# Even units regrouped in a fused attention loop: scores, one dV quarter, gradient products, then o and dQ; q transposes for dK in halves

## The chip, the cores and the metric

The kernel runs on one core of a Trainium2 chip. The metric is device time in microseconds (us): 1098.23 us, the median of three runs of the kernel before (1097.64 to 1101.65).

## The reference, cut to what matters

The reference returns the output of two attention blocks side by side and the gradients of all inputs for a given `grad_out`. Block A is linear attention. Block B, whose work fills the loop that is changed, is softmax attention with 16 query heads of width 28 that share one key and one value head, over 2048 tokens:

```python
q = (x @ wq).reshape(B, S, H, Dh)     # transposed to heads first
k = x @ wk
v = x @ wv
scores = jnp.einsum("bhqd,bkd->bhqk", q, k) * (Dh ** -0.5)
p = _softmax(scores, axis=-1)
o = jnp.einsum("bhqk,bkd->bhqd", p, v)
...                                    # o @ wo, and the vjp of all of it for grad_out
```

So the loop needs, for each pair of heads and each stretch of queries, the exponentiated scores, o, the product of the gradient of o with v, the gradient of the scores (dS), and from these dQ, dK and dV.

## The kernel before

A first stage of about 205 us does block A and the projections of block B. The loop in the middle does the attention of block B, and a last stage of about 40 us does the remaining weight and input gradients.

**Tiling of the loop.** A *block* b (64 of them) is a pair of heads with 256 queries; eight blocks share one query chunk `qc`. A *unit* u (512 of them, `NU`) is an eighth of a block: two tiles of 128 keys (t2 = 0, 1), both heads (h = 0, 1). The loop runs over u and is written under `tc.manual_schedule()`, so every engine and every queue runs its instructions in the order in which the loop writes them. A unit works on several stages at once, on older and older data:

- `rows_SD` (lines 683 to 705): score products S of unit u into two of three banks `SB`, and products D of the gradient with v for unit w = u - 16 into the two banks `DB`. Each has four matmuls of 32 rows. They lie on different rows of the TensorE array: 32 rows each for S of h = 0 and 1 and for D of h = 0 and 1.
- ScalarE: `eT` = exp(S) for h = 0 (line 939), the copy `cp` of D for h = 1 (line 953), exp(S) for h = 1 (line 985), in this order.
- VectorE: `dsT` = D * eT for h = 0 (line 951), and the 32x32 transpose `dsx` of the dsT of unit u - 18 (line 1023). GpSimd: dsT = cp * eT for h = 1 (line 954).
- The SyncE queue (SP): in every odd unit one DMA transpose of two units of `eT` into `eN` (line 988), 16 blocks of 128x128. The ring `ETs` holds 20 units, `ENs` 24.
- TensorE, at the end of a unit: in odd units `dk_m` (dK, 32 matmuls on 32x32 tiles, with `dsx` and `qX`), in even units `o_dq` (o of units u - 2, u - 1 and dQ of units u - 20, u - 19, 16 matmuls) and after it `dv_mm` (dV). `dv_mm` (line 894) does a quarter of a block's dV, eight matmuls that read `eN` of the whole block. For block b the quarters 0 and 1 come in unit 8b + 20, quarter 2 in 8b + 22, quarter 3 in 8b + 24, and none in 8b + 26.
- Every eight units there are a few more: `onat_T`, `o_norm`, `row_D`, `don_T`, `don_copy`, and a slice of the output projection (`out_proj`), which borrow the third SB bank (`spare`).

**q for dK.** For each query chunk from 1 to 7, `qc_copy` (line 842, GpSimd) spreads a group of q rows into the one buffer `qst` in two copies, and `qc_T` (line 847, SP queue) transposes it into `qX`, 8 blocks of 128x128. This happens four times per 64 units, for u mod 64 in 30 to 58: the copies are written in units 30 and 31, 38 and 39, 46 and 47, 54 and 55, and `qc_T` at the end of units 31, 39, 47 and 55, behind that unit's `eN` transpose. Since `qst` is one buffer, the copies of units 38, 46 and 54 wait until the DMA of the `qc_T` before has landed.

**The first twenty units.** `do_proj` and `do_copy` do the first ten row tiles of the gradient projection in units 1, 3, ..., 19. Units below 16 use a DB bank, 17 and 19 the bank `dk_acc`, which dV and dK use from unit 20 on.

Of the kernel before, what the change touches and what calls it, by code (L numbers as in the profile page):

```python
# [17 lines left out]
P = 128  # L18
# [7 lines left out]
def kernel(  # L26
# [21 lines left out]
    nc = tc.nc  # L48
# [31 lines left out]
    def mm(out_ap, lhsT, rhs, start=True, stop=True):  # L80
        nc.tensor.matmul(out_ap, lhsT=lhsT, rhs=rhs, start=start, stop=stop, tile_position=(0, 0))  # L81
# [565 lines left out]
    NB = 64  # L647
# [3 lines left out]
    with ExitStack() as cs_:  # L651
# [10 lines left out]
        DB = [psA.tile([P, 512], F32, name="agen") for i in range(2)]  # L662
        oq, dk_acc = (psA.tile([P, 512], F32, name="agen") for _ in range(2))

        dsT, dsx, qX, don, doT, rl, prod = ({} for _ in range(7))
# [3 lines left out]
        def eT(u):  # L669
            return ETs[u // 4 % 5][:, u % 4, :, :]  # L670

        def eN(b, c):
            return ENs[(2 * b + c // 2) % 6][:, 16 * (c % 2):16 * (c % 2) + 16, :]

        def mmt(out, lhsT, rhs, pos, start, stop):
            nc.tensor.matmul(out, lhsT=lhsT, rhs=rhs, start=start, stop=stop, tile_position=pos,  # L676
                             skip_group_check=True)

        def blk(b):
            qc, pair = divmod(b, 8)  # L680
            return qc, pair, pair // 2, pair % 2

        def rows_SD(u, sp, dp):
            b, tp = divmod(u, 8)
            w = u - 16
            qc, pair, g, hp = blk(b)
            todo = [(0, 0), (0, 1), (1, 0), (1, 1)] * 2
            if sp is not None and dp is not None and u % 2 == 0:
                todo = [(0, 0), (0, 1), (1, 0)] * 2 + [(1, 1)] * 2
            seen = {}  # L690
            for d in todo:
                if (dp if d[0] else sp) is None:
                    continue
                k, h = d
                t2 = seen.get(d, 0)
                seen[d] = 1
                t = 2 * tp + t2
                tc_ = slice(t * P, (t + 1) * P)
                oc = slice(t2 * 256, (t2 + 1) * 256)
                r = 64 * (1 - hp if k else hp) + 32 * h  # L700
                if k:
                    mmt(dp[h][:, oc], vT_rep[r:r + 32, tc_], doT[w // 8][r:r + 32, :], (r, 0), True, True)
                else:
                    mmt(sp[h][:, oc], kT_rep[r:r + 32, tc_], qT_B[g][r:r + 32, qc * 256:(qc + 1) * 256],
                        (r, 0), True, True)
# [3 lines left out]
        qst = pp_.tile([P, 8, 4, 32], BF16, name="qst", bufs=1)[:, :, :, :]  # L709
# [85 lines left out]
        def due(u, lag):  # L795
            b, r = divmod(u - lag, 8)
            return b if r == 0 and 0 <= b < NB else None
# [46 lines left out]
            eng.tensor_copy(out=st.rearrange("p (b s) a j -> p b s a j", s=2)[:, :, s, :, :],  # L844
                            in_=src.unsqueeze(2).to_broadcast([P, 4, 4, 32]))

        def qc_T(st, qc, g):
            nc.sync.dma_start_transpose(qX[qc].rearrange("p b s c -> p (b s) c")[:, :, g * P:(g + 1) * P],
                                        st.rearrange("p n a j -> p (n a j)"))

        KH = 256
        kv_acc = [dk_acc]
# [1 line left out]
        def dk_quad(a, x):  # L854
            return 32 * ((a + 2 * x) % 4)

        def dk_m(b, m):
            qc, pair, g, hp = blk(b)
            h, B, s = m // 8, (m // 2) % 4, m % 2
            for x in range(2):  # L860
                for a in range(4):
                    rhs = dsx[b][32 * a:32 * a + 32, 4 * x:4 * x + 4, h, :, :].rearrange(
                        "p u t (b i s) -> p u t b i s", b=4, s=2)[:, :, :, B, :, s]
                    k = dk_quad(a, x)
                    mmt(kv_acc[x][k:k + 32, 0:KH],
                        qX[qc][32 * a:32 * a + 32, B, s, pair * 64 + 32 * h:pair * 64 + 32 * h + 32],
                        rhs, (32 * a, k), False, b == NB - 1 and m == 15)
# [19 lines left out]
        def o_dq(vs, ys):  # L887
            for v, y in zip(vs, ys):
                todo = [f(i) for f, i in ((o_mm, v), (dq_mm, y)) if 0 <= i < NU]
                for _ in range(2):  # L890
                    for g_ in todo:
                        next(g_)

        def dv_mm(b, h, qb):
            for x in range(2):
                for c in range(4):
                    rhs = eN(b, c).rearrange("p (u h t q) k -> p u h t q k", u=2, h=2, t=2)[:, x, h, :, qb, :]
                    mmt(kv_acc[x][32 * c:32 * c + 32, KH:512], don[b][:, qb, h, :], rhs, (0, 32 * c),
                        b == 0 and h + qb == 0, b == NB - 1 and h + qb == 2)

        def do_proj(i, c0, c1, ps):
            for c in range(4):
                mm(ps[:, 0:c1 - c0], gbT[:, i, c, :], woTp[:, c, c0:c1], start=(c == 0), stop=(c == 3))
# [1 line left out]
        def do_copy(i, c0, c1, ps):  # L905
            nc.vector.tensor_copy(out=do_nat[:, i, c0:c1], in_=ps[:, 0:c1 - c0])

        do_slots = {2 * i + 1: (i, 0, 512) for i in range(10)}
        do_slots.update({37 + 8 * (n // 2) + 2 * (n % 2): (10 + n // 4, n % 4 * P, n % 4 * P + P) for n in range(24)})
        with tc.manual_schedule():  # L910
            nc.sync.dma_start(wo, wo_d[:, 0:D].rearrange("(g p) c -> p g c", p=P))
            qX[0] = pqa_.tile([P, 4, 2, 512], BF16, name="qX")
            for g in range(4):
                st = pd_.tile([P, 2, 512], BF16, name="dsT").rearrange("p a (n j) -> p a n j", j=32).rearrange(
                    "p a (n b) j -> p (a n) b j", b=4)
                qc_copy(nc.gpsimd, st, 0, g, 0)
                qc_copy(nc.vector, st, 0, g, 1)
                qc_T(st, 0, g)
            for u in range(NU + 28):
                w = u - 16  # L920
                hasS = u < NU
                hasD = 0 <= w < NU
                sp = [SB[(2 * u + h) % 3] for h in range(2)] if hasS else None
                dp = DB if hasD else None
                spare = SB[(2 * u + 2) % 3] if hasS else DB[u // 4 % 2] if u > 530 else SB[2]
                rows_SD(u, sp, dp)
                if (b := due(u, 10)) is not None:
                    onat_T(b, spare)
                if (b := due(u, 14)) is not None:
# [2 lines left out]
                    out_proj(*op, spare)  # L932
                dpj = do_slots.pop(u, None)
                if dpj is not None:
                    dps_ = DB[u // 2 % 2] if u < 16 else dk_acc if u < 20 else spare
                    do_proj(*dpj, dps_)

                if hasS:
# [16 lines left out]
                gq, iq = divmod(u % 64 - 30, 8)  # L955
                qq = u // 64 + 1
# [11 lines left out]
                if (b := due(u, 27)) is not None:  # L968
                    qc, pair, g, hp = blk(b)
# [14 lines left out]
                if hasS:  # L984
                    nc.scalar.activation(out=eT(u)[:, 1, :], in_=sp[1][:, :], func=ACT.Exp, scale=scale)  # L985
                    if u % 2:
                        k = u % 4 - 1
                        nc.sync.dma_start_transpose(ENs[u // 4 % 6][:, 8 * k:8 * k + 16, :],
                                                    ETs[u // 4 % 5][:, k:k + 2, :, :].rearrange("p a b c -> p (a b c)"))
                    if 0 <= gq < 4 and iq == 1 and u < 448:  # L990
                        qc_T(qst, qq, gq)

                if u % 2:
                    b, i = divmod(u - 27, 8)
                    if 0 <= b < NB:
                        for m in range(2 * i, 2 * i + 4):
                            dk_m(b, m)
                else:
                    o_dq((u - 2, u - 1), (u - 20, u - 19))
                    b, n = divmod(u - 20, 8)  # L1000
                    for k in {0: (0, 1), 2: (2,), 4: (3,)}.get(n, ()) if 0 <= b < NB else ():
                        dv_mm(b, k // 2, k % 2)
                y = u - 18

                if 512 <= u < 528 and u % 2 == 0:
# [13 lines left out]
                if 0 <= y < NU:  # L1019
                    b, tp = divmod(y, 8)  # L1020
# [19 lines left out]
        for c in range(4):  # L1040
            for x in range(2):
                k = dk_quad(c, x)
# [100 lines left out]
```

## Time and profile before

| | |
|---|---|
| median of three runs | 1098.23 us |
| the profiled execution | 1102.18 us |
| its span, first to last instruction | 1100.4 us |
| mean granted TensorE clock | 0.973 |
| TensorE matmul busy | 1011.5 us (92%) |
| VectorE busy | 902.7 us (82%) |
| ScalarE busy | 879.3 us (80%) |
| GpSimd busy | 799.4 us (73%) |
| DMA packets of the SP and ACT transposes and copies (queue q1) | 684488, 179.99 MB |

The profiled execution took 3.95 us more than the median, and 1.8 us of it lie outside its span. The busy shares are averages over three stages; in the loop ScalarE and VectorE are above 90%. A matmul's end is modelled, so a busy TensorE is not one at its peak. The SP queue has no busy row on the page: its instructions only issue DMAs, and their durations stand in the timeline of that queue.

### The profile page before, as it was taken

To read this page: it belongs to the slowest core of one execution; us is meant where nothing else is said; L and a number is where in the kernel's file an instruction comes from. 1 tells how busy PE (TensorE), PEld (TensorE's weight loads), DVE (VectorE), ACT (ScalarE), POOL (GpSimd) and SP (SyncE) were. 2 spreads that over 40 slices of the span, in tenths; PEclk is the share of its full clock that TensorE was granted. 3 is DMA by queue.
4 is the path that set the end of the run, shared out by engine and by line. 5 is a ranking of instruction groups with operands and counts; after the bars stand their busy time and mean duration, and the time that the engine had idled before them with its cause. 6 is when DMAs were issued, how large, how long until landed. Compare 5 with 4: busy or idle time off the path is not lost.

```text
span 1100.4 us, 49383 instructions
## 1 busy us (share of the span) xinstructions
PE 1011.5 (92%) x20717; PEld 555.8 (51%) x20717; DVE 902.7 (82%) x1794; ACT 879.3 (80%) x1745; POOL 799.4 (73%) x1044
## 2 busy tenths in 40 slices
PE   9999999989999889989988998999899989999898
PEld 5655554444555545545554554455455544555444
DVE  7895503578999989989998998899899978999942
ACT  6553223799999989989998998899989978999532
POOL 8501451368888888878888888888898878888851
PEclk9999999999999999989999899899999989999999
DMA  9879998499999999999999999999999999999993
GB/s 259 151 146 189 204 213 165 91 173 177 181 179 175 180 185 179 175 182 187 171 181 182 182 186 178 175 186 184 175 178 189 172 185 184 185 169 178 225 169 91
DMA packets 693193, 195.77 MB, mean 178 GB/s; under 512 B 674505, under 2 KB 690785, under 8 KB 692969
## 3 DMA queue, kind: packets, MB, share of 16 engines
q1 hardware_dynamic: 684488, 179.99, 105.2%
q0 software_dynamic: 4544, 9.46, 3.4%
q10 hardware_dynamic: 3936, 3.16, 0.9%
q8 instruction: 162, 2.65, 0.9%
q14 instruction: 63, 0.51, 0.1%
HBM read 12.60 MB, written 10.84 MB: 21 GB/s over the span
## 4 chain that ended last, share of the span: by engine, by line
PE 35%; ACT 19%; issue 16%; DVE 16%; POOL 10%; SPq 2%; DMA 1%; DVEq 0%; ACTq 0%; POOLq 0%
PE agen L81 12%; ACT cp L953 10%; PE agen L676 8%; POOL dsT L954 8%; ACT eT L985 7%; PE aacc L676 6%; PE aacc L81 6%; DVE dsx L1023 5%; DVE dsT L951 4%; DVE oTs L967 2%; DVE oTs L812 1%; ACT eT L939 1%; PE aacc L833 1%; DVE rl L811 1%; SPq L1014 1%
## 5 line engine op out<-in xcount | busy, mean ns | idle before, releaser
L954 POOL TENSOR_TENSOR dsT<-cp,eT 128x512 bf16<-128x512 bf16 x512 | 587.7, 1157 | 79.2 <-ACT cp L953 72.4
L1023 DVE STREAM_TRANSPOSE dsx<-dsT 128x512 f32<-128x512 f32 x512 | 358.3, 700 | 24.4 <-POOL dsT L954 22.2
L676 PEld LDWEIGHTS <-R 32*128 32x128 bf16 (+1 forms) x8192 | 233.7, 94 | 285.6 <-issue 255.5
L951 DVE TENSOR_TENSOR dsT<-agen,eT 128x512 bf16<-128x512 f32 x512 | 342.4, 669 | 26.6 <-PE agen L676 20.8
L939 ACT ACTIVATE eT<-aacc 128x512 bf16<-128x512 f32 x512 | 311.5, 608 | 43.0 <-PE agen L676 30.9
L953 ACT ACTIVATE cp<-agen 128x512 bf16<-128x512 f32 x512 | 312.3, 610 | 23.0 <-PE agen L676 12.7
L985 ACT ACTIVATE eT<-aacc 128x512 bf16<-128x512 f32 x512 | 318.2, 621 | 0.0
L676 PE MATMUL aacc<-R,R 32*128 32x256 bf16 x2048 | 255.6, 280 | 32.6 <-DVE oTs L812 26.5
L676 PE MATMUL agen<-doT,R 32*128 32x256 bf16 x2048 | 272.1, 275 | 12.7 <-DVE dsT L951 2.8
L676 PE MATMUL agen<-dsT,R 128*32 128x256 bf16 x2048 | 165.3, 283 | 7.9 <-POOL dsT L954 7.7
L676 PE MATMUL aacc<-dsx,qX 32*32 32x256 bf16 x4096 | 170.2, 279 | 0.1
L676 PE MATMUL agen<-dsx,qX 32*32 32x256 bf16 x4096 | 169.8, 279 | 0.0
L676 PE MATMUL agen<-eT,R 128*32 128x256 bf16 x2048 | 164.3, 282 | 0.1
L676 PEld LDWEIGHTS <-qX 32*32 32x32 bf16 x8192 | 93.9, 90 | 55.6 <-issue 51.8
L81 PEld LDWEIGHTS <-R 128*128 128x128 bf16 x781 | 60.7, 97 | 59.3 <-issue 24.3
L676 PE MATMUL agen<-eN,don 128*32 128x256 bf16 x1024 | 80.3, 287 | 0.0
L676 PE MATMUL aacc<-eN,don 128*32 128x256 bf16 x1024 | 80.2, 286 | 0.0
L844 POOL COPY qst<-R 128x512 bf16<-128x512 bf16 x56 | 34.2, 611 | 50.5 <-DMA qX<-qst 50.5
L676 PEld LDWEIGHTS <-don 128*32 128x32 bf16 x2048 | 64.6, 102 | 3.4
L81 PE MATMUL agen<-R,R 128*128 128x448 bf16 (+1 forms) x168 | 39.0, 359 | 0.7 <-ACT R L229 0.4
L816 POOL TENSOR_TENSOR prod<-R,oTs 128x128 f32<-128x128 bf16 x64 | 27.6, 431 | 9.3 <-DVE oTs L812 9.3
L586 DVE TENSOR_TENSOR osb<-R 32x512 bf16<-32x512 bf16 x4 | 1.7, 413 | 34.9 <-ACT R L583 34.9
(237 smaller groups left out, 1010.1 us busy)
## 6 DMA issues: line engine op xcount, KB each, us to landing
eN<-eT SPq DMA_TRANSPOSE x256
xa<-in_A_x_dram SPq DMA_DIRECT2D x8, 224.0 KB
ga<-in_grad_out_dram SPq DMA_DIRECT2D x4, 448.0 KB
out_dram<-osb ACTq DMA_DIRECT2D x16, 112.0 KB
xa<-in_grad_out_dram POOLq DMA_DIRECT2D x4, 448.0 KB, 10.1
out_dram<-wdq POOLq DMA_DIRECT2D x8, 224.0 KB, 5.4
eT<-in_grad_out_dram SPq DMA_DIRECT2D x4, 448.0 KB
eT<-in_B_x_dram SPq DMA_DIRECT2D x4, 448.0 KB
```

What stands on the lines that cost most here:

```text
L81: nc.tensor.matmul(out_ap, lhsT=lhsT, rhs=rhs, start=start, stop=stop, tile_position=(0, 0))
L676: nc.tensor.matmul(out, lhsT=lhsT, rhs=rhs, start=start, stop=stop, tile_position=pos, skip_group_check=True)
L811: nc.vector.reciprocal(out=r_[:], in_=onp[:, :, :, 0:1])
L816: nc.gpsimd.tensor_tensor(out=prod[b][:], in0=dnv, in1=os_, op=ALU.mult)
L844: eng.tensor_copy(out=st.rearrange("p (b s) a j -> p b s a j", s=2)[:, :, s, :, :], in_=src.unsqueeze(2).to_broadcast([P, 4, 4, 32]))
L939: nc.scalar.activation(out=eT(u)[:, 0, :], in_=sp[0][:, :], func=ACT.Exp, scale=scale)
L951: nc.vector.tensor_tensor(out=dst[:, 0, :], in0=dp[0][:, :], in1=ew[:, 0, :], op=ALU.mult)
L953: nc.scalar.activation(out=cp[:, :], in_=dp[1][:, :], func=ACT.Copy)
L954: nc.gpsimd.tensor_tensor(out=dst[:, 1, :], in0=cp[:, :], in1=ew[:, 1, :], op=ALU.mult)
L967: nc.vector.tensor_copy(out=oTs[0:64, :], in_=oq[0:64, 0:256])
L985: nc.scalar.activation(out=eT(u)[:, 1, :], in_=sp[1][:, :], func=ACT.Exp, scale=scale)
L1023: nc.vector.transpose(out=dsx[b][:, tp, :, :, :].rearrange("p h t c -> p (h t c)").bitcast(F32), in_=dsT[y][:, :, :].rearrange("p h c -> p ...
```

## The change

In even units in which both S and D exist (u = 16 to 510), `rows_SD` is called twice: first for S alone, in the order h = 0, 1, 0, 1, then one quarter of dV, then `rows_SD` for D alone, 0, 1, 0, 1. Before, these units had the order S0 S1 D0, S0 S1 D0, D1 D1, and dV came last. The quarters of block b now lie one each in units 8b + 18, 20, 22 and 24 (`dv_due`). Odd units stay S0 S1 D0 D1, twice.

`qc_T` takes a range of the eight blocks. It is called twice per group, with four blocks each, at the end of the even units that follow by one and by three: 32 and 34, 40 and 42, 48 and 50, 56 and 58 (mod 64). The copies stay where they are.

In the first units, `do_proj` moves to 1, 3, 5, 7, 9, 11, 13, 14, 15, 17, with `dk_acc` in 14 and 17, so that `dk_acc` is free when dV begins in unit 18.

```diff
-            if sp is not None and dp is not None and u % 2 == 0:
-                todo = [(0, 0), (0, 1), (1, 0)] * 2 + [(1, 1)] * 2
...
-        def qc_T(st, qc, g):
-            nc.sync.dma_start_transpose(qX[qc].rearrange("p b s c -> p (b s) c")[:, :, g * P:(g + 1) * P],
-                                        st.rearrange("p n a j -> p (n a j)"))
+        def qc_T(st, qc, g, n0=0, n1=8):
+            nc.sync.dma_start_transpose(qX[qc].rearrange("p b s c -> p (b s) c")[:, n0:n1, g * P:(g + 1) * P],
+                                        st[:, n0:n1, :, :].rearrange("p n a j -> p (n a j)"))
...
+        def dv_due(u):
+            b, n = divmod(u - 18, 8)
+            if 0 <= b < NB:
+                dv_mm(b, n // 4, n // 2 % 2)
...
-        do_slots = {2 * i + 1: (i, 0, 512) for i in range(10)}
+        do_slots = {u: (i, 0, 512) for i, u in enumerate((1, 3, 5, 7, 9, 11, 13, 14, 15, 17))}
...
-                rows_SD(u, sp, dp)
+                split = hasS and hasD and u % 2 == 0
+                if split:
+                    rows_SD(u, sp, None)
+                    dv_due(u)
+                    rows_SD(u, None, dp)
+                else:
+                    rows_SD(u, sp, dp)
...
-                    dps_ = DB[u // 2 % 2] if u < 16 else dk_acc if u < 20 else spare
+                    dps_ = dk_acc if u in (14, 17) else DB[u // 2 % 2] if u < 16 else spare
...
-                    if 0 <= gq < 4 and iq == 1 and u < 448:
-                        qc_T(qst, qq, gq)
+                    if 0 <= gq < 4 and iq in (2, 4) and u < 448:
+                        qc_T(qst, qq, gq, 2 * iq - 4, 2 * iq)
...
-                    b, n = divmod(u - 20, 8)
-                    for k in {0: (0, 1), 2: (2,), 4: (3,)}.get(n, ()) if 0 <= b < NB else ():
-                        dv_mm(b, k // 2, k % 2)
+                    if not split:
+                        dv_due(u)
```

## The prediction

> **What bounds the kernel now.** I read the page first. ScalarE and VectorE stand at 80% and 82% of the span, but the loop is only three quarters of it. The table by stretch gives the loop, here one stretch outside and one inside the units that prepare q for dK. Columns: length, then busy us of TensorE, weight loads, VectorE, ScalarE, GpSimd, the granted clock, DMA share, GB/s.
>
> ```profile
> 308.50:357.40 48.90, 45.00 (x1200) 26.16 (x1192) 47.58 (x96) 48.03 (x96) 42.10 (x51) 1.00 1.23 181
> 571.00:620.00 49.00, 43.31 (x1068) 23.08 (x1068) 43.05 (x83) 43.39 (x86) 40.18 (x49) 0.90 1.17 175
> ```
>
> In the first, ScalarE is busy for 48.03 of 48.90 us and eight units take 12.2 us. In the second, ten instructions of ScalarE fewer fit into the same time. From the starts of line 939, the stretches of eight units from u mod 64 = 40, 48 and 56 take 15.4, 13.1 and 13.8 us, all others 12.1 to 12.3: 5.7 us lost per 64 units, 40 us over seven chunks. What is waited for there is in the groups and the timeline:
>
> ```profile
> L844 POOL COPY qst<-R 128x512 bf16<-128x512 bf16 x56 | 34.2, 611 | 50.5 <-DMA qX<-qst 50.5
> ```
>
> ```profile
> 601.86 0.61 POOL L844 COPY qst<-R 128x512 bf16<-128x512 bf16 x1 [2.77 <-DMA qX<-qst]
> ...
> 603.62 0.71 DVE L1023 STREAM_TRANSPOSE dsx<-dsT 128x512 f32<-128x512 f32 x1 [1.23 <-POOL dsT L954]
> ...
> 605.99 0.60 ACT L939 ACTIVATE eT<-aacc 128x512 bf16<-128x512 f32 x1 [1.29 <-DVE dsx L1023]
> ```
>
> GpSimd waits for the landing of the transpose that read `qst` (21 times, 2.4 us on average), VectorE then for GpSimd, ScalarE for VectorE. Of the 50.5 us, 40 are lost. So why is that DMA late? The copies of units 30 and 31 end at 561.5 us, their transpose is issued at 570.1, with ScalarE in unit 38. The SP queue's own timeline says why:
>
> ```profile
> 574.62 9.63 SPq L988 DMA_TRANSPOSE eN<-eT  x3
> 584.35 1.26 SPq L848 DMA_TRANSPOSE qX<-qst  x1
> 585.71 11.54 SPq L988 DMA_TRANSPOSE eN<-eT  x4
> 597.34 1.50 SPq L848 DMA_TRANSPOSE qX<-qst  x1
> 598.95 11.22 SPq L988 DMA_TRANSPOSE eN<-eT  x4
> 610.26 2.05 SPq L848 DMA_TRANSPOSE qX<-qst  x1
> ```
>
> There is no gap. From unit 30 to 510 transposes fill 743.8 of 773.7 us, and most of the rest is the 0.1 us between two. Each `eN` transpose is issued 5 to 11 us, mostly 8, after its exp has ended. This **lag** neither grows nor vanishes. In stretches without `qX`, one `eN` transpose takes 3.02 us of the queue (12 of them in 36.2 us), the compute 3.05 us per two units: about even. A `qX` transpose adds 1.40 us (the stretch from unit 29 to 65 holds 18 and four, 59.96 us). So the queue needs 32 x 3.02 + 4 x 1.40 = 102.2 us per 64 units, with the few transposes of line 976 about 103; the compute alone needs 97.6; the loop takes 103.2. My reading: the queue is the bound, and the waits at `qst` are the place where the compute is held back to its pace.
>
> Behind the queue, the trace's packet records show the transposes' packets stopping for about 1.2 us whenever one of the 162 packets of 16 KB of queue q8 (instruction fetch, 1.0 us each) passes, as at 529.3 and 533.6 us. TensorE's instruction count does not change, so neither does this.
>
> **Part by part.**
>
> *qX in halves, the queue's time.* 28 issues become 56. Short ones have a floor:
>
> ```profile
> L988 SPq DMA_TRANSPOSE eN<-eT x256: 1705/2969/4225, 213.6 to 1031.3; - x128
> ...
> L848 SPq DMA_TRANSPOSE qX<-qst x28: 1252/1262/2365, 262.4 to 921.8; - x28
> ...
> L109 SPq DMA_TRANSPOSE blks<-R x4: 1192/1242/1368, 27.3 to 31.3; - x4
> ```
>
> (min/median/max ns.) Sixteen blocks take 2.97 us, eight 1.26, and four, in the first stage, still 1.24. Upper bound: each half costs this floor and the gap of 0.1, a pair 2 x 1.3 = 2.6 instead of 1.40, times 28: +34 us. Lower bound: the queue only waits for the engines, and cost goes with blocks; the line through 16 blocks (3.02) and 8 (1.40) gives 0.59 for four, 1.18 a pair: -6 us. Between them the backlog decides. When a `qX` transpose is issued, mostly 900 to 1500 packets issued earlier have not started (128 a block), and the engines start some 700 per us. A half puts nothing new in for about 1.2 us (in the first stage its packets start that much after its issue), which the backlog covers; but it brings only 512, so the 1.3 us before the next `eN` transpose delivers may run dry for some 0.2 us. That is nearer the lower end: 0.45 us more per pair, 28 x 0.45 = **+13 us**.
>
> The Trainium skill, "Perfetto Trace Analysis", section What "DMA-bound" means, says that a sequencer track of solid DMA slices is bound on descriptor generation and not on data; by that rule the halves would cost their floor, the upper sum. The backlog in the row above speaks against taking it whole.
>
> *qX in halves, their place.* The second half now stands behind the `eN` transpose of the next odd unit: +3.0 us, less some 0.3 for its shorter flight (the whole lands 4.3 us after issue on average). If the lag stayed, the 21 waits would grow by 2.7 us each, 57 us. It cannot stay: time lost by the compute is time in which the queue catches up. The lag settles about 2.7 us lower and the waits again sum to what the queue needs. Once 2.7 us, and nothing at the end, where the chain of waits holds 6.51 us for the `grad_out` loads that stand behind the last transposes: less lag shortens that. **0**, 57 if the lag did not fall. No other wait joins SP's queue: the halves wait for copies that end far earlier.
>
> *Even units, rows.* S and D lay on different array rows and started three or four at a time every 0.11 us. Now they go in pairs: four passes, not three, +0.11 us of TensorE in 248 units (27 us). In the calm stretch, D for h = 1 ends 0.4 us before `cp` starts in even units; D for h = 0 now stands behind D of h = 1 and may come 0.1 to 0.3 us later, which `dsT` of VectorE feels in units 0 and 6 mod 8, where it starts 0.15 us after it: at most 0.3 us per eight units. The slack against the queue is (103.2 - 97.6) / 8 = 0.7 us per eight units, so this hides: **0**; without that cover 0.3 x 62 = 19 us. The Trainium skill, "TensorE: Matmul & The Clock Gate", Part 3, says that matmuls on distinct row groups run at once and gives up to 3.07 times for four; by it alone, pairs instead of fours in a stream that TensorE bounds, the change would cost those 27 us of passes. Behind D are queued `onat_T`, `don_T`, `out_proj` and o_dq, and through the spare bank S of the next unit.
>
> *dV quarters.* Unit 4 mod 8 takes 1.59 us with two quarters, unit 6 1.48 with one: evening out is worth 0.11 x 62 = 7 us of compute, which only turns into a longer wait at `qst`: **0**, -7 at best. New is that dV's first quarter comes two units earlier. The last `eN` it reads lands on average 1.6 us before S of that unit starts; in 10 of 62 blocks it would have been late, 12 us together, all by less than 2.6 us. With 2.7 us less lag none is: **0**, 12 if the lag stays. Behind a late one stand D, o and dQ on TensorE, and then VectorE and `cp`.
>
> *First units.* Two `do_copy` move by one or two units, and dV of unit 18 waits for the copy of unit 17 once: under 1.5 us, which the lag of 8 us takes.
>
> Sum: 1102.18 + 13 = 1115 for the profiled execution, which was 3.95 above the median: 1098.23 + 13 = 1111.
>
> **The rivals.** A measurement of this kernel can tell about 0.5%, 5.5 us, from no change.
>
> - *The full floor.* Every half costs the issue floor: +34, 1132. For it: 16 of 28 `qX` transposes sit at 1.26, the floor, with backlog behind them. Against: `eN` transposes can shrink to 1.7 us afterwards.
> - *Nothing.* The engines set the pace, blocks cost what they cost: 0, 1098, with the bounds -5 to +5.
> - *Faster.* The queue only follows. In units 3 to 9, where the scores run alone, it issued `eN` transposes every 2.3 to 2.5 us with a lag of 5.3 to 5.5, again just the compute's pace. If its pace rises with the compute's, the balanced dV counts (-7), and half of ScalarE's 30.9 us of waits before line 939 for TensorE may go in even units, since S no longer stands behind D0 and its bank: together up to -22, I take -12, 1086. It decides when `eN` transposes take under 2.9 us in the calm stretches. Against: 0.1 us gaps all through.
> - *The lag does not fall:* +57 and some, 1155. Against: in chunk 6 a wait of 6.4 us brought the lag from 13 to 7.
>
> **How the numbers follow.** Forecast (5 to 25 more) 0.46, full floor 0.11, lag stays 0.03: slower 0.60. Nothing: same 0.25. Faster 0.15. The range reaches from 1092, inside the faster case, to 1132, the floor; the forecast's own is 1104 to 1124.
>
> **What would show it.** Right: 56 `qX` transposes of about 1.2 us each on a queue without gaps; `eN` lag 2 to 3 us lower in later chunks; GpSimd's wait at `qst` at 55 to 75 us; eight calm units still 12.1 to 12.3; no wait of dV for a DMA. Wrong: gaps in the SP queue, a calm pace under 12.0 us, waits at `qst` near 100, or matmuls of dV waiting for `eN`.

## The result, and the profile after

The changed kernel takes 1130.41 us, the median of four runs (1126.81 to 1135.22); beside it on the same chip the kernel before took 1097.93 (four runs, 1095.71 to 1101.65). The ratio is 1.0295, 95% interval 1.0246 to 1.0344: **slower by 32.5 us**, where +13 was forecast. The profiled execution took 1129.29 us with a span of 1127.6, against 1102.18 and 1100.4 before, so the two traces that are compared here differ by 27 us: the one before was 3.95 us above its median, the one after 1.1 below. In the later comparisons, on three chips, the kernel before had medians of 1102.28 to 1103.19.

First the queue that the prediction named as the bound. The SP queue's instructions by line, durations as min/median/max in ns:

```profile
L997 SPq DMA_TRANSPOSE eN<-eT x256: 1713/2896/4544, 214.2 to 1058.4; - x128
...
L846 SPq DMA_TRANSPOSE qX<-qst x56: 1201/1446/2579, 262.1 to 951.4; - x56
```

The last `eN` transpose is issued at 1058.4 us, 27.1 later than before (1031.3), and what follows it is as long as before (69.2 us to the end of the span, 69.1 before). So all of the difference arises ahead of that issue. The same 50 us of the SP timeline as in the prediction:

```profile
573.56 9.15 SPq L997 DMA_TRANSPOSE eN<-eT  x3
582.82 1.22 SPq L846 DMA_TRANSPOSE qX<-qst  x1
584.14 2.60 SPq L997 DMA_TRANSPOSE eN<-eT  x1
586.79 1.79 SPq L846 DMA_TRANSPOSE qX<-qst  x1
588.68 7.75 SPq L997 DMA_TRANSPOSE eN<-eT  x3
596.52 2.03 SPq L846 DMA_TRANSPOSE qX<-qst  x1
598.66 3.00 SPq L997 DMA_TRANSPOSE eN<-eT  x1
601.71 1.27 SPq L846 DMA_TRANSPOSE qX<-qst  x1
```

There is no gap in these lines either. A half of four blocks takes 1.2 to 2.0 us here (1.45 in the median of all 56), as long as a whole transpose of eight did. The `eN` transposes between two halves are somewhat shorter than 3 us (2.58 on average), but not by as much as the halves add. What queue q1 moves is the same: 179.99 MB in both kernels, in 685384 packets after and 684488 before.

Then the compute. One stretch of 32 units, 64 to 96, in both traces, the one before first (columns as in the prediction's table):

```profile
304.74:354.04 49.30, 45.40 (x1212) 26.54 (x1216) 47.98 (x97) 48.43 (x97) 41.99 (x50) 1.00 1.20 177
```

```profile
311.88:365.00 53.12, 47.57 (x1212) 24.41 (x1216) 48.33 (x97) 49.57 (x97) 42.06 (x50) 1.00 1.19 180
```

The same work takes 3.8 us more, 13.28 per eight units in place of 12.33, at the full clock, and ScalarE, which filled 98% of the stretch before, now has 3.55 us of idle time. TensorE's busy time grew by 2.17 us in 16 even units. So the engines also became slower. In calm stretches after unit 128, from start of exp to start of exp, eight units (a "calm eight" below, by medians) take 12.45 us (12.17 before), and units 2 and 6 mod 8 are the ones that grew (1.83 and 1.68 us, from 1.68 and 1.50). How unit 142 (6 mod 8) hands over to 143, on TensorE and VectorE of the kernel after:

```profile
439.35 0.29 PE L676 MATMUL agen<-eN,don 128*32 128x256 bf16 x4
439.47 0.28 PE L676 MATMUL aacc<-eN,don 128*32 128x256 bf16 x4
439.69 0.39 PE L676 MATMUL agen<-doT,R 32*128 32x256 bf16 x4
...
441.18 0.28 PE L676 MATMUL aacc<-R,R 32*128 32x256 bf16 x2 [0.43 <-DVE doT L838]
```

```profile
440.11 0.69 DVE L960 TENSOR_TENSOR dsT<-agen,eT 128x512 bf16<-128x512 f32 x1
440.83 0.29 DVE L838 COPY doT<-aacc 64x256 bf16<-64x256 bf16 x1
```

The dV quarter (two lines with `eN,don`) runs before D. D ends late, `dsT` (L960) starts late, `doT` stands behind it, and S of the next unit waits 0.43 us for the bank that `doT` frees. In the list of waits (total, times, longest) these are:

```profile
DVE dsT L960 <- PE agen L676: 43.4, 80, 1.3
...
PE aacc L676 <- DVE doT L838: 19.7, 54, 0.5
```

Before:

```profile
DVE dsT L951 <- PE agen L676: 20.8, 59, 1.3
...
PE aacc L676 <- DVE doT L840: 0.6, 3, 0.2
```

And the wait that carried the prediction, GpSimd's at `qst`:

```profile
L842 POOL COPY qst<-R 128x512 bf16<-128x512 bf16 x56 | 34.1, 610 | 51.4 <-DMA qX<-qst 48.0 <-DVE dsT L960 3.4
```

It is 48.0 us, 2.5 less than before, though the kernel lost 27 us. Two things happened at once, so they have to be tried one by one.

### The profile page after: what moved, and what is told of

Read it like the earlier page. It is cut to its first block, busy times and chain, and to the rows that moved or that the text cites. A ratio compares the mean times of both kernels' runs of the same rounds, so it can differ in the third digit from the quotient of the medians.

```text
span 1127.6 us, 49433 instructions
## 1 busy us (share of the span) xinstructions
PE 1021.8 (91%) x20710; PEld 514.9 (46%) x20717; DVE 908.6 (81%) x1794; ACT 888.9 (79%) x1745; POOL 800.0 (71%) x1044
## 3 DMA queue, kind: packets, MB, share of 16 engines
q1 hardware_dynamic: 685384, 179.99, 102.9%
## 5 line engine op out<-in xcount | busy, mean ns | idle before, releaser
L963 POOL TENSOR_TENSOR dsT<-cp,eT 128x512 bf16<-128x512 bf16 x512 | 587.8, 1156 | 105.3 <-ACT cp L962 71.3
L960 DVE TENSOR_TENSOR dsT<-agen,eT 128x512 bf16<-128x512 f32 x512 | 345.4, 675 | 54.1 <-PE agen L676 43.4
L676 PEld LDWEIGHTS <-R 32*128 32x128 bf16 (+1 forms) x8192 | 225.1, 95 | 324.5 <-issue 302.4
L676 PE MATMUL aacc<-R,R 32*128 32x256 bf16 x2048 | 241.4, 279 | 63.0 <-DVE oTs L810 31.7
L676 PE MATMUL agen<-doT,R 32*128 32x256 bf16 x2048 | 207.3, 279 | 16.0 <-DVE dsT L960 12.3
L676 PEld LDWEIGHTS <-qX 32*32 32x32 bf16 x8192 | 94.2, 90 | 56.7 <-issue 52.3
L81 PEld LDWEIGHTS <-R 128*128 128x128 bf16 x781 | 56.9, 97 | 54.2 <-issue 23.9
L676 PE MATMUL aacc<-eN,don 128*32 128x256 bf16 x1024 | 76.7, 281 | 0.0
L676 PEld LDWEIGHTS <-don 128*32 128x32 bf16 x2048 | 33.6, 95 | 55.3 <-issue 55.0
```

The lines of the kernel that those rows point to most:

```text
L960: nc.vector.tensor_tensor(out=dst[:, 0, :], in0=dp[0][:, :], in1=ew[:, 0, :], op=ALU.mult)
L963: nc.gpsimd.tensor_tensor(out=dst[:, 1, :], in0=cp[:, :], in1=ew[:, 1, :], op=ALU.mult)
```

## The experiments

The kernels were tried in three groups, each on one chip and beside runs of the kernel before there (medians 1102.28, 1103.19 and 1102.63 us). To read them, one table was made from the traces: the time between the starts of two `eN` transposes on the SP queue, for three stretches of units, with the number of `qX<-qst` transposes issued in it. A stretch of the queue is a better measure than one of the compute, since it does not depend on how the lag changes.

| kernel | 1 to 97 | 97 to 161 | 161 to 447 | last `eN` issue, us |
|---|---|---|---|---|
| before | 151.0 (5) | 105.3 (4) | 463.1 (19) | 1031.3 |
| after | 155.1 (9) | 107.8 (8) | 482.3 (39) | 1058.4 |
| halves alone | 155.3 (9) | 107.8 (8) | 483.0 (39) | 1058.6 |
| halves back to back | 159.6 (10) | 109.3 (8) | 483.1 (38) | 1066.3 |
| 28 more transposes | 156.4 (9) | 108.0 (8) | 489.7 (38) | 1067.3 |
| new order, whole | 157.9 (5) | 104.3 (4) | 462.5 (19) | 1036.9 |
| whole, three units later | 152.0 (4) | 103.2 (4) | 465.0 (20) | 1033.1 |
| groups 10 units apart | 152.2 (5) | 105.4 (4) | 460.1 (19) | 1031.2 |
| new order, dV last, whole | 150.2 (5) | 105.6 (4) | 462.9 (19) | 1030.6 |
| dV quarters evened alone | 152.4 (5) | 104.2 (4) | 464.7 (19) | 1032.3 |

**The halves alone.** The kernel before with `qc_T` as in the change (it takes a range of blocks) and

```diff
-                    if 0 <= gq < 4 and iq == 1 and u < 448:
-                        qc_T(qst, qq, gq)
+                    if 0 <= gq < 4 and iq in (2, 4) and u < 448:
+                        qc_T(qst, qq, gq, 2 * iq - 4, 2 * iq)
```

Expected: 

> The kernel before, with only the q transposes cut in halves and moved to the even units, as in the change. Theory 1 (the SyncE queue of DMA transposes bounds the loop): the changed kernel's trace gives 2.29 us of queue per pair where the whole took 1.40, so +0.89 x 28 = +25 us, about 1123, and the eight calm units stay at 12.2 us. Rival (the new order of the even units costs the time): at most +5, and the halves change nothing that can be measured.

Measured: 1130.05 us, ratio 1.025 (1.0211 to 1.0289), +27.8 us. The calm eight stays at 12.17 us, so here only the queue grew, and the wait at `qst` took it up:

```profile
L844 POOL COPY qst<-R 128x512 bf16<-128x512 bf16 x56 | 34.1, 610 | 76.8 <-DMA qX<-qst 75.3 <-DVE ot L740 1.5
```

That is the upper end of the 55 to 75 us that the prediction gave for this wait, and the mechanism it named. The price is the other: 20 transposes more between units 161 and 447 make 19.9 us, 1.0 us for each added issue.

**The order alone.** The kernel after with `qc_T` whole and in odd units, as before.

```diff
-                    if 0 <= gq < 4 and iq in (2, 4) and u < 448:
-                        qc_T(qst, qq, gq, 2 * iq - 4, 2 * iq)
+                    if 0 <= gq < 4 and iq == 1 and u < 448:
+                        qc_T(qst, qq, gq)
```

Expected: 

> The changed kernel, with the q transposes whole and at the odd units as before; all of the new order of the even units stays. Theory 1: the calm units get slower (12.2 to 12.5 us per eight, units 2 and 6 of eight by 0.16 and 0.18 us), but eight units still take less than the 12.9 us that the queue needs, so only the first chunk and a half, where eight units took 13.3, shows: +3 to +8 us. Rival: +20 to +28, the calm loss of 0.3 us per eight units x 62 and the first chunk's.

Measured: 1108.12 us, ratio 1.0065 (1.0035 to 1.0094), +5.8 us by the medians. The calm eight is 12.45 us as in the kernel after, but from unit 161 to 447 the queue needs 462.5 us, no more than before. The loss sits in units 1 to 97 (+6.9 us): there the slower engines let the queue run empty (the lag at unit 29 is 0.6 us, 6.7 before). Its timeline shows it as a block that is too long for its transposes (14 in 46.44 us, 3.32 each, gaps included; before, 8 in 24.23 us, 3.03 each):

```profile
323.99 46.44 SPq L997 DMA_TRANSPOSE eN<-eT  x14
```

The trace shows two things in it. In units 16 to 40 the granted TensorE clock is low: 0.70, 0.50 and 0.84 in the three stretches of eight units (before, 1.00, 0.87 and 1.00), which take 46.9 us together (37.8 before). And from unit 40 to 128, at a clock of 1.00, eight units take 13.2 to 13.4 us, 0.9 us more than stretches without a wait at `qst` took before (12.25 to 12.45), not 0.3. Up to unit 127 the loop also does the last 24 slices of the gradient projection (`do_slots`). Why the clock is lower, and whether these slices make the order dearer, was not tried, so how the loss divides between clock and order is not shown.

Later the lag is built up again, from 2.5 us at unit 161 to 5.9 at unit 447, and the slower order costs nothing more; GpSimd's wait at `qst` falls to 20.7 us.

**One transpose more per group of units, where nobody waits.** If the queue is the bound, a transpose that no engine waits for costs its full time. The kernel before with

```diff
+                    if u % 64 in (57, 59, 61, 63) and u < 448:
+                        qc_T(qst, qq, 3)
```

Expected: 

> The kernel before, with the transpose of the last q group of each chunk issued four more times (28 in all, same data to the same place) in units 57 to 63, where no copy waits for it. Theory 1: each costs the queue its 1.40 us, and the loop has to follow: +39 us, about 1137. Rival: nobody waits for these transposes, so 0 to +5 us.

Measured: 1139.81 us, ratio 1.0348 (1.0299 to 1.0397), +37.5 us, 1.34 for each of 28. The queue takes them one after the other between `eN` transposes that keep their length:

```profile
625.82 3.87 SPq L988 DMA_TRANSPOSE eN<-eT  x1
629.78 1.27 SPq L848 DMA_TRANSPOSE qX<-qst  x1
631.16 3.17 SPq L988 DMA_TRANSPOSE eN<-eT  x1
634.42 1.26 SPq L848 DMA_TRANSPOSE qX<-qst  x1
```

This shows the main reading: work put on this queue alone, with no consumer of its own, comes out in full. The rival of a queue that only follows the engines falls. What the run does not separate is issuing from moving, since a whole transpose more brings its packets too. The packet records help there. From unit 161 to 447 this kernel starts 335873 of the transposes' packets of 256 bytes, the kernel before 316105, and both need 1.46 us per 1000 (all kernels with whole transposes, 1.45 to 1.47). The three kernels with halves start as many as the kernel before and need 1.53.

**Groups further apart.** The kernel before with the four groups ten units apart, not eight, so that the transpose before has two units more to land.

```diff
-                gq, iq = divmod(u % 64 - 30, 8)
+                gq, iq = divmod(u % 64 - 30, 10)
```

Expected: 

> The kernel before, with the four groups of q spread 10 units apart instead of 8 (units 30, 40, 50, 60 mod 64). The queue's work is the same; the copies that wait for the landing of the transpose before come 3 us later. Theory 1: the waits vanish at first, the lag of the queue grows by some 3 us, and they come back: -3 us, 1095. Rival (the wait is the latency of that one transfer and no sign of a full queue): the 40 us lost there go almost wholly, 1060 to 1070.

Measured: 1102.11 us, ratio 0.9999 (0.9977 to 1.0021). The wait at `qst` falls from 50.5 to 19.4 us, the lag rises to 8 to 13 us (6 to 10 before), and nothing is won: the wait was only the place where the pace was held. From unit 97 to 511 GpSimd's waits at `qst` fell by 27 us, those before `dsT` for `cp` rose by 22 (52.3 to 74.2). The expected -3 lies just outside the interval (-2.5 to +2.3) and is not seen.

**Halves back to back.** Is the price of a half that of its issue, or does it come from the place between two `eN` transposes? The kernel before, with `qc_T` as in the change and both halves at the place of the whole:

```diff
                     if 0 <= gq < 4 and iq == 1 and u < 448:
-                        qc_T(qst, qq, gq)
+                        qc_T(qst, qq, gq, 0, 4)
+                        qc_T(qst, qq, gq, 4, 8)
```

Expected: 

> The kernel before, with each q transpose cut in two halves that are issued back to back where the whole one was (units 31, 39, 47, 55). Theory A (the price of a half is its issue time of about 1.2 us and the gap, whatever stands between): a pair costs 2.3 to 2.6 us of queue where the whole took 1.40, so +25 to +34 us, as with the halves apart. Theory B (the halves cost because each is followed by an eN transpose that finds the engines' backlog short): back to back the pair costs little more than the whole, +0 to +10.

Measured: 1134.62 us, ratio 1.0295 (1.027 to 1.0319), +31.4 us. The two halves of a pair together (timeline of its SP queue):

```profile
588.02 2.54 SPq L848 DMA_TRANSPOSE qX<-qst  x2
590.66 12.12 SPq L988 DMA_TRANSPOSE eN<-eT  x4
602.87 2.54 SPq L848 DMA_TRANSPOSE qX<-qst  x2
605.51 11.42 SPq L988 DMA_TRANSPOSE eN<-eT  x4
```

These pairs take 2 x 1.27 us, on a queue that ran 8 to 13 us behind the exps (6 to 10 in the kernel before). They are near the shortest of the 28, 2.51 us; the median is 3.0. So each issue takes at least its 1.2 us, however few blocks it brings.

**The whole transpose, three units later.** It stands where the second half of the change stood in even units (`iq == 4` in place of `iq == 1`), in one piece.

Expected: 

> The kernel before, with the whole q transpose issued three units later (end of units 34, 42, 50, 58), behind one more eN transpose. Theory 1 (the queue's work counts, not the place): each wait at first grows by some 3 us, the lag of the queue settles 3 us lower, the time is the same, -2 to +3 us. Rival (the place counts): 21 waits longer by 2.7 us, +40 to +57.

Measured: 1104.26 us, ratio 1.0014 (0.9997 to 1.0031), +1.1 us. After unit 97 the lag fell from 6 to 10 us to 4 to 7, and the waits at `qst` stayed (51.1 us). So the place of the transpose costs nothing that these runs can tell, as the prediction said of the halves' place, and the rival of a lag that does not fall is refuted.

**The order without the dV quarter in it.** What slows the even units: S and D in pairs, or the quarter between them? The kernel after with whole transposes and

```diff
                 if split:
                     rows_SD(u, sp, None)
-                    dv_due(u)
                     rows_SD(u, None, dp)
...
-                    if not split:
-                        dv_due(u)
+                    dv_due(u)
```

Expected, of a single run and then of the timed ones: 

> The new order of the even units, q transposes whole, but the dV quarter stays at the end of the unit instead of between S and D. If D's delay by the dV quarter is what slows units 2 and 6 of eight, the calm eight units go back from 12.45 to 12.15-12.25 us and the time to 1098-1103; if it is the pairing of D for h = 0 and 1, they stay at 12.4 to 12.5.

> The change's order of even units without the dV quarter between S and D (the quarter stands at the unit's end; one quarter each in units 8b+18, 20, 22, 24), whole qX transposes, now timed. The look at this order showed a calm eight of 12.17 us, as in the kernel before. If the queue of transposes alone sets the pace of the loop, calm units and even dV counts change nothing: -3 to +2 us. Rival: taking the second quarter out of unit 4 mod 8 is worth some of the 7 us of compute also under the queue: -7 to -4 us.

Measured: 1100.14 us in the single run; timed 1102.75, ratio 1.0004 (0.9985 to 1.0023). The calm eight is back at 12.17 us, and both waits are back at the size of the kernel before:

```profile
DVE dsT L959 <- PE agen L676: 18.8, 61, 1.2
...
PE aacc L676 <- DVE doT L838: 0.9, 4, 0.3
```

So S and D in pairs cost nothing that these runs can tell; the quarter ahead of D does. That even dV counts would be worth some us under the queue is not seen.

**Only the dV quarters evened.** The order of `rows_SD` as before, `dv_due(u)` at the end of the even units, `do_proj` moved to match.

Expected: 

> The kernel before with only the dV quarters evened out: one at the end of each of the units 8b+18, 20, 22, 24, and the gradient projections of the first units moved to match; order S0 S1 D0 D1 as before, whole qX transposes. Queue theory: -2 to +2 us, since neither the transposes nor their number change. Rival (the first quarter, two units earlier, now waits for late eN): +5 to +12 us, with TensorE waits for the eN transposes of about 12 us.

Measured: 1104.28 us, ratio 1.0014 (0.9994 to 1.0035). TensorE's matmuls wait for `eN` transposes 2.0 us in all (three times), so the 12 us that the prediction kept as its worst end are out, and so is a gain: unit 4 mod 8 takes 1.54 us with one quarter or with two.

**Less on the queue.** Three tries for a faster version, the diff of the second below: the eight small DMAs of `put_shift` (unit 11) and the 14 copies of unit 532 on GpSimd in place of SP; only `put_shift`, and in unit 5; and that with the order without dV in it.

```diff
-                if u == 11:
+                if u == 5:
                     for n in (2, 3):
-                        put_shift(nc.sync, shifts[n], slice(n * 512, n * 512 + 512))
+                        put_shift(nc.gpsimd, shifts[n], slice(n * 512, n * 512 + 512))
```

Expected, of the first: 

> The kernel before, with two groups of small copies issued by GpSimd instead of SyncE: the eight shift rows of unit 11 (4.6 us of the queue in which no eN transpose is issued) and the 14 small copies of unit 532 (7.3 us in the chain that ends last). Theory 1: every microsecond taken off the queue is won: -4 us from the first, up to -7 from the second, 1087 to 1094 against 1098. Rival (the queue is not the bound in the loop, or GpSimd's issue takes as long at the end): -1 to +2.

Of the second: 

> The kernel before with the eight small DMAs of put_shift issued by GpSimd in unit 5, where it has nothing to do, instead of by SP in unit 11. SP's queue is relieved of their issues. If the queue sets the pace from the first units on, and the issues on GpSimd stand before nothing, the loop gets shorter by about 4 us: -5 to -2 us. Rival: the queue has slack in units 10 to 30 and nothing comes of it: -1 to +1 us.

Of the third: 

> split_no_dv and shift_early together: a candidate for the fastest version. If both theories hold, the sum of the two runs alone, -7 to 0 us, most likely -4; if the pace of the compute after unit 10 is what is left, no more than split_no_dv alone.

Measured: 1105.66 us, ratio 1.0026 (1.0009 to 1.0043), a miss; 1102.72, ratio 0.9993 (0.9977 to 1.0009); 1101.14, ratio 0.9984 (0.9972 to 0.9996). In the first, GpSimd's issues stand in front of `don` (L825), with which the first D begins; its timeline, with L825 at 222.12 us in the kernel before:

```profile
221.69 4.48 POOL L632 DMA_DIRECT2D R<-R  x8
226.19 0.23 POOL L825 TENSOR_TENSOR don<-Dq,rl 128x4 bf16<-128x4 f32 x1
231.58 1.15 POOL L954 TENSOR_TENSOR dsT<-cp,eT 128x512 bf16<-128x512 bf16 x1 [5.17 <-ACT cp L953]
```

The first product with D starts at 231.58 us, 3.73 later than before (227.85), of which 0.8 lay ahead of these issues already (L816 starts at 220.61 us, 219.79 before). Even so this trace has units 1 to 97 in 149.9 us of the queue (151.0 before) and a span of 1099.5, so the late start does not account for the miss, whose cause stays open. In the second the trace shows units 1 to 97 in 147.8 us of the queue (151.0 before) and a span of 1097.2, but over twelve runs the gain is not told from none. The third is the fastest against the kernel before beside it, by 1.8 us (0.4 to 3.1), less than a measurement of this kernel can well tell.

## Why the prediction was right, and where it was wrong

**The bound: right.** The queue of transposes sets the pace from unit 161 to 447. All kernels there with whole transposes in the usual number, the new order or the old, the groups near or far, need 460 to 465 us of it; all with halves need 482 to 483. An idle transpose costs its full 1.34 us. The kernel after leaves this pace once: behind 12 us at a granted clock of 0.55 (735 to 747 us) the lag is at most 0.6 us from unit 321 to 349, the queue has six gaps of 0.4 to 1.2 us there, and units 321 to 353 take 51.3 us of it (49.2 with the halves alone).

**The price of a pair: wrong, and it is the main miss.** The prediction took 0.45 us more per pair, 13 in all, between -6 and +34. From unit 161 to 447 of the kernel after, the queue took 19.2 us more for 20 issues more, 0.96 each: 28 x 0.96 = 27 us, and 27.1 is what the traces differ by. The step that failed is the 1.2 us of a half "which the backlog covers". In that stretch the `qX` transposes take 32.1 us more (28.2 before, 60.3 after), so each added issue pays 1.6 us; the `eN` transposes give back 17.4 (410.9 to 393.6), about half, and the time in no transpose grows by 5.1. The prediction let 0.75 of the floor's 1.2 us per pair come back; here 1.6 is paid and 0.96 stays. The upper bound (1.2 per pair more) was nearer, and with it the rival that every half costs the full floor, as the back-to-back run shows with 20.0 us for 19 issues there. The backlog itself was there: when a half is issued in the kernel after, 644 to 1581 packets issued earlier have not started. It did not keep the engines fed. Counted in steps of 0.1 us, the time in which fewer than ten of the transposes' packets start is 112 us before, 122 after, 128 with the halves alone and 124 with them back to back: 10 to 16 us more, 0.5 to 0.8 for each added issue.

The Trainium skill, "Perfetto Trace Analysis", section What "DMA-bound" means, whose rule of a solid sequencer track the prediction weighed and set aside, was the better guide for the halves: by it a pair costs its floor, 1.2 us more than the whole, and here it cost 0.96 to 1.05 more. For whole transposes the runs do not show whether issuing or the packets set the 1.46 us per 1000. Why the `eN` transposes give back half and not all was not tried and stays open.

**The place of the halves: right.** The lag fell where it was to fall (on average at unit 29 mod 64: 4.3 us, from 7.7; at unit 61: 5.1, from 6.5), and the whole transpose three units later cost +1.1 us (-0.3 to +3.4).

**Even units: the cost where it was put, its cover only where the queue is behind.** "Calm units still 12.1 to 12.3" failed: 12.45. The 0.3 us per eight units is there, but from the dV quarter in front of D and in units 2 and 6, not from S and D in pairs; the prediction had dV's move at 0 for VectorE and looked only at what dV waits for. The slack of 0.7 us per eight units covers it after unit 161. Before unit 97 it does not: alone, the order loses 6.9 us there. From unit 40 on eight units take 0.9 us more there and not 0.3, and ahead of that the granted clock fell, to 0.50 in units 24 to 32. With the halves in place the queue is slower anyway in that stretch (155.3 us without the new order, 155.1 with it), so by the traces the order adds nothing in the kernel after; by the medians it could add up to some 5 us (27.8 alone against 32.5 for both, with intervals that overlap). That remains open.

The Trainium skill, "TensorE: Matmul & The Clock Gate", Part 3, was weighed there too: pairs on distinct row groups in place of fours, 27 us by its rule alone. The passes do not show. With S and D in pairs, dV last and whole transposes, TensorE is busy for 44.91 us of units 64 to 96 (45.40 in the kernel before), and the time is +0.4 us (-1.7 to +2.5). The 2.17 us that it is busy longer in the kernel after come with the dV quarter between S and D: with whole transposes and that order it is 47.57 us too.

**dV quarters and first units: right in sum.** In the kernel after, TensorE waits for an `eN` transpose once, 0.4 us. Evening the counts is worth nothing, also as compute. The first 30 units take 3 us more with dV evened (44.9, from 42.0), twice the 1.5 of the prediction. In units 16 to 32, where two of the 3 us lie, the granted clock was lower (0.85 and 0.67 by eights, 1.00 and 0.87 before), so how much of it is the change's is open. The lag took up most (152.4 us of the queue up to unit 97, from 151.0; 150.2 with dV last).

**The waits at `qst`:** 55 to 75 us were expected. In the kernel after it is 48.0, since the slower even units now use up part of the slack; with the halves alone it is 75.3. The new order takes as much off it with whole transposes (20.7, from 50.5).

## What to carry to other kernels

A queue whose timeline has no gaps and whose lag stays even is a bound like an engine: add up what its instructions take, and look at what the shortest one there takes before one is split in two, since the same bytes in more instructions can cost more. A backlog behind such a queue is no proof that it covers a short issue. To see what a wait at such a queue's consumer is worth, put one more transfer on the queue that nobody waits for: if it costs its full time, shortening or moving the wait alone will win nothing. Where a bound covers a slower order, look at every stretch for itself, at its granted clock too: here the order cost more than the slack in the first hundred units, used up the lag, and came out there.

## What the runs showed of the hardware

A DMA transpose of four blocks of 128x128 took at least 1.19 us of the SP queue, and in the median 1.26 when issued in pairs and 1.38 to 1.45 between `eN` transposes; one of eight blocks took 1.26, one of 16 took 2.9 to 3.0. From unit 161 to 447 the queue needed 1.45 to 1.47 us per 1000 packets of 256 bytes with whole transposes, in eleven traces, and 1.53 with halves, in three. With a backlog the `eN` transpose that follows a half is shorter (2.35 us on average behind two halves back to back, 2.79 behind a whole), so part of the issue time comes back, but in no run all of it.
